# Another order for the first 24 steps of a fused clustered-attention and expert kernel

## The chip, the cores and the metric

The kernel runs on one core of a Trainium2 chip. The metric is the device time of one execution, in microseconds (us). Five queues of instructions run side by side, each strictly in order: TensorE (PE in the profile, its weight loads PEld), VectorE (DVE), ScalarE (ACT), GpSimd (POOL) and SyncE (SP, which here only issues transfers). SPq and ACTq in a row stand for a transfer being issued by that engine's queue.

## The reference, cut to what matters

```python
q_assign = argmax(q_n . c_n)   # 16 clusters a head; k_assign likewise
mask = q_assign[:, :, :, None] == k_assign[:, :, None, :]
scores = where(mask, q k^T / sqrt(D), -1e9)
attn = softmax(scores) @ v                 # 4 batches, 8 heads, 768 tokens, D = 64
x = attn as 3072 rows of 512
out = top-2-of-8 gated experts(x, w1, w2)  # 512 -> 1024 -> 512, relu
```

q, k and the centroids are normalised for the assignment alone.

## The kernel before, in words

Attention is done for 16 pairs of heads, in 192 score steps: pair p, head s of the pair, block kc of 128 keys is step 12p + 6s + kc. A step's `scores` makes two tiles of 128 keys x 384 queries on TensorE (operands A and B, one after the other into the same tile) and has ScalarE take the exponential of each; `split_p` has GpSimd make the second half of the result; `values` multiplies with v four to nine steps later. The score tiles, and those of most helpers, are the six buffers `ring` of PSUM; the seventh writer waits for the reader of the first.

Ahead of its first score a pair needs a preparation, called *pair work* here:

- `scales`: two sums of squares of q and k (ScalarE), a floor, a spread over partitions (TensorE) and a last part of five VectorE instructions that gives the powers of two to scale by. The list holds them in this order.
- `a_turn` and `a_halves` (together `a_split`), four times: three transposes on TensorE, then a high half (ScalarE) and a low half (VectorE) of the turned q or k, into the tile `hl`. That tile has one buffer for pairs 0, 2, 3 and on; pair 1 alone uses another one.
- `b_place`: ten transfers that copy parts of hl into the operands A[p % 3] and Bt[p % 3].
- `a_sims`: 36 short matmuls of the halves with the centroids `wh`, into the tile `aux`; five VectorE instructions on it (`max1`, `ge`, `ky`, `max2`, `eq`) that end in a one-hot; `a_mask`, which turns that on TensorE and writes `mk` from ScalarE; and `b_mask`, four transfers of mk into rows of A, two on SP's queue and two on ScalarE's. 
- `b_max`, for each of twelve row blocks: two matmuls and two VectorE reductions of 128 x 384 that give minus the largest masked score; `b_neg`, three short VectorE instructions, which use columns of `aux` too; and `b_negT`, a transpose, a ScalarE copy and a transfer into Bt. Pair 0 does b_neg and b_negT for each of its heads, the other pairs once for both.

The pair's scores need A with its mask and Bt with its maxima. `load_qk` loads q and k of four heads (two pairs) at a time; `load_v`, `v_sizes`, `v_scale` and `v_split` do the like for v.

The order of all of this is written by hand. `at(step, f)` files f under a third of a step, rounded to the nearest; within one third the order is that in which the calls were filed. A loop then goes through the steps from the first negative one on and issues, in each: what was filed for the first third, the step's `scores`, a `split_p`, the second third, `values`, and the last third. This order is the order on every queue. The times come from the table `AT`, by pair: `first` for pair 0 and offsets (`sec`, `thr`, `place1`, `scales1`, `bmax1`) for pairs 1 and 2. Before, the preparation of pairs 0 and 1 and most of that of pair 2 stands ahead of step 0: pair 2's squares at step -14, its a_split from -5.2 to -3, its b_place at -1.2, pair 1's mask at -12.1 and three row blocks of b_max of pair 0's second head ahead of step 0 or in its first third.

After attention the experts run (lines 949 to 1288), TensorE's matmuls L1230 and L1270 above all.

Of the kernel before, what the change touches and what calls it, by code (L numbers as in the profile page):

```python
# [9 lines left out]
F32 = mybir.dt.float32  # L10
# [4 lines left out]
AF = mybir.ActivationFunctionType  # L15
OP = mybir.AluOpType
# [9 lines left out]

AT = dict(
    ahead=6,
    first={'scales': [-6.667] * 5, 'place': -2.333, 'sims': [-3.333, -2.667], 'max1': -2.333, 'ge': -2.333, 'max2': -2.333, 'eq': -1.333, 'mask': -1.0, 'bmask': -1.0, 'ky': -2.333, 'split': [-5.333, -5.0, -5.333, -4.0], 'bmax': [3.667, 22.667], 'bstep': [1.0, 0.667], 'neg': [9.0, 26.667], 'negT': [9.333, 27.333]},
    L=4, qk=-20.667, v=-8.667,  # L30
    vscale=-0.667, vsplit=10.667, vstep=1.0, split=[-4.667, -3.667, -4.0, -3.333], place=-0.667,
    sims=[2.0, 2.667], scales=[-14.333, -13.333, -13.0, -10.0, -8.667], scales1=2.0, max1=3.333, ge=3.667, max2=4.333, eq=4.667, mask=6.333, bmask=6.333,
    bmax=9.333, neg=20.333, negT=22.0, zero=31.0, zstep=12.0, zlist=21.0, v1=4.0, store=2.667, turn=6.667, glog=12.0,
    xh=1.333, xh0=4.0, pause=4.0, list=[34.0, 34.0, 19.0], lstep=[2.0, 2.0, 1.1667], bstep=1.0,
    gate=[13.667, 13.667, 6.333], am=5.333, amstep=0.333, xs=6.0, ky=4.0, cut=[13, 20], gplace=[30.0, 30.0, 14.333],
    vd=[1, 1, 2, 3, 4, 5], sec=-6.0, qf=[0, -4.0], place1=4.333,
    fv=[{'v': -5.0, 'vscale': 13.0, 'am': 24.333, 'amstep': 0.333, 'vsplit': 25.333, 'vstep': 2.0},
        {'v': 9.0, 'vscale': 11.667, 'am': 13.333, 'amstep': 0.333, 'xs': 14.0, 'vsplit': 15.0, 'vstep': 1.0}],
    wmax=42, thr=0.333, bmax1=14.667, bstep1=0.5)


def rap(tensor, offset, dims):
# [3 lines left out]
class Kernel:  # L46
# [171 lines left out]
    def centroids(self):  # L218
        nc, D, C = self.nc, self.D, self.C
        self.early = self.wk.tile([128, 2, 384], F32, name="pe", bufs=6).rearrange("p a n -> p (a n)")  # L220
        o = 128 + 4 * C
        c1 = self.early[:, o:o + D]
        c2 = self.c2 = self.early[:, o + D:o + 3 * D].rearrange("p (a d) -> p a d", d=D)
        nc.sync.dma_start(c1, self.cent.rearrange("h c d -> (h c) d"))
        self.constants()
        n = self.early[:, o + 3 * D:o + 3 * D + 3]
        nc.vector.tensor_mul(c2[:, 0, :], c1, c1)
        nc.vector.reduce_sum(n[:, 0:1], c2[:, 0, :], axis=X)
        self.rnorm(n[:, 0:1], n[:, 1:3])
        nc.vector.tensor_scalar(c2, c1[:, None, :].to_broadcast([128, 2, D]), n[:, 0:1], None, op0=OP.mult)  # L230

    def c_turn(self):
        nc, H, C = self.nc, self.H, self.C
        HC = H * C
        p = self.ps()
        nc.tensor.transpose(p[:, :128], self.c2.rearrange("p a d -> p (a d)"), self.ident)
        for a in range(2):
            r = slice(64 * a, 64 * a + 64)
            src = p[r, :HC].rearrange("p (h c) -> p h c", c=C)
            hi, lo = (self.wh[r, :, i, C * a:C * a + C] for i in range(2))  # L240
            nc.scalar.activation(hi, src, AF.Copy, scale=64.0)
            nc.vector.scalar_tensor_tensor(lo, src, 64.0, hi, op0=OP.mult, op1=OP.subtract)
        self.early = self.c2 = None

    def attention(self, ctx):
        nc, tc = self.nc, self.tc
        B, H, S, D, NJ = self.B, self.H, self.S, self.D, self.NJ
# [9 lines left out]
        NP = B * H // 2  # L257
# [8 lines left out]
        def at(step, f, *a):  # L266
            sched.setdefault(divmod(round(3 * step), 3), []).append((f, a))
# [6 lines left out]
        T = AT  # L274
        for p in range(NP):
            b, hp = divmod(p, H // 2)
            w = 12 * (p - 2)
            if hp == 0:
                for g in range(2):
                    at(w + T["qk"] + 24 * g + (0 if b else T["qf"][g]), self.load_qk, b, g)  # L280
                    v = w + 24 * g
# [4 lines left out]
                    if g:  # L286
                        fs = self.x_scale(b)
                        chain(v + V["xs"] - (4 if b else 0), 1.0 if b else 0.333, fs[:-1])
                        at(v + V["xs"] + (2.667 if b else 3.333), fs[-1])
                    for h in range(0, 4, 2):  # L290
                        at(v + V["vsplit"] + V["vstep"] * (h + 0.667), self.v_split, b, g, h)
            P = T["first"] if p == 0 else T
            w += (0, T["sec"], T["thr"])[p] if p < 3 else 0
            if p == 0:
                for i in range(4):
                    at(w - 7.0, self.a_turn, p, i // 2, i % 2)
            if p < 2 or p % 2 == 0:
                fs = self.scales(p, 2 if p < 2 else 4)
                for x, f in zip(P["scales"], fs):
                    at(w + x + (T["scales1"] if p == 1 else 0), f)  # L300
            for i in range(4):
                at(w + P["split"][i], self.a_halves if p == 0 else self.a_split, p, i // 2, i % 2)
            if p == 0:
                at(w + P["sims"][0], self.c_turn)
            at(w + P["place"] + (T["place1"] if p == 1 else 0), self.b_place, p)
            for s in range(2):
                at(w + P["sims"][s], self.a_sims, p, s)
            for k, f in (("max1", self.a_max1), ("ge", self.a_ge), ("ky", self.a_ky), ("max2", self.a_max2),
                         ("eq", self.a_eq), ("mask", self.a_mask), ("bmask", self.b_mask)):
                at(w + P[k], f, p)  # L310
            if p == 0:
                for s in range(2):
                    for j in range(NJ):
                        at(w + P["bmax"][s] + P["bstep"][s] * j, self.b_max, p, s, j)
                    at(w + P["neg"][s], self.b_neg, p, s, 1)
                    at(w + P["negT"][s], self.b_negT, p, s, 1)
            else:
                w = 12 * (p - 2)
                bm, bs = (T["bmax1"], T["bstep1"]) if p == 1 else (T["bmax"], T["bstep"])
                for s in range(2):  # L320
                    for j in range(NJ):
                        at(w + bm + bs * (6 * s + j), self.b_max, p, s, j)
                at(w + T["neg"], self.b_neg, p, 0, 2)
                at(w + T["negT"] + (T["thr"] if p == NP - 1 else 0), self.b_negT, p, 0, 2)
            w = 12 * (p - 2)
            z = w + 36 + L
            if p + 1 < NP:
                at(z + T["xh"] + (T["xh0"] if p == 0 else 0), self.x_halves, p)
                at(z + T["store"] + (T["xh0"] if p == 0 else 0), self.store_x, p)
                turn, glog = (T["store"], 6.333) if p == NP - H // 2 - 1 else (T["turn"], T["glog"]) if p < NP - 2 else (5.0, 8.0)  # L330
# [3 lines left out]
            if hp == H // 2 - 1:  # L334
                if b + 1 == B:
                    continue
                fs = self.g_gate(b)
                chain(z + T["gate"][b], 0.333, fs[:8])
                for i, f in enumerate(fs[8:self.GP]):
                    x = T["gate"][b] + 2.667 + (0.333 if b < 2 else 0.1667) * i  # L340
# [3 lines left out]
                    at(z + T["list"][b] + T["lstep"][b] * j, self.g_list, b, j)  # L344
        at(17.667, self.x_early)
        at(T["zlist"], self.zero_list)
        at(-13, self.exp_table)
        at(10.667, self.load_gate)
        chain(13.667, 0.667, self.gate_halves())
        for i in range(self.N // 256):  # L350
# [18 lines left out]
            at(z - 7 + i, self.turn_x, 0, i)  # L369
        at(z - 8, self.open_x)  # L370
        for i in range(2):
            nc.gpsimd.memset(self.oh[i], 0.0)
        nc.gpsimd.memset(self.nm, 0.0)
        self.fixed_init(0)
        at(-14.4, self.fixed_init, 1)
        at(-8.4, self.fixed_init, 2)
        self.at = at
        for t in range(min(sched)[0], z + L + 2):
            u = t - L
# [8 lines left out]
            if 0 <= u < z:  # L388
                p, s, kc = u // 12, (u % 12) // 6, u % 6
# [5 lines left out]

    def fixed_init(self, i):
        nc = self.nc
        nc.gpsimd.memset(self.A[i][64:96], 0.0)
        nc.gpsimd.memset(self.Bt[i][96:128], 0.0)
        nc.gpsimd.memset(self.Bt[i][96:98, 0], 1.0)  # L400
        nc.gpsimd.memset(self.Bt[i][96:97, 0], MASK)

# [181 lines left out]
    def b_place(self, p):  # L584
        hl, A, Bt = self.st[p]["hl"], self.A[p % 3], self.Bt[p % 3]
        for a in range(2):
            r = 64 * a
            cs = slice(384 * a, 384 * a + 384)

            self.dma(A[0:64, :, :, cs], hl[r:r + 64, 1:3])  # L590
            self.dma(A[96:128, 0, :, cs], hl[r:r + 32, 3])
            self.dma(A[96:128, 1, :, cs], hl[r:r + 32, 2])
            self.dma(Bt[0:64, :, :, cs], hl[r:r + 64, 0:2])
            self.dma(Bt[64:96, :, :, cs], hl[r + 32:r + 64, 2:4])

# [735 lines left out]
```

## Time and profile before

| | |
|---|---|
| Median of three runs | 1013.66 us (1013.41 to 1014.27) |
| The profiled execution's own time, and its span | 1013.59 us, 1011.8 us |
| Mean granted TensorE clock | 0.976 of full speed |
| Busy share of the span | PE 92%, DVE 65%, ACT 47%, POOL 56% |
| First exponential of step 0, step 24 | 44.79 us, 100.18 us |

Times in rows count from the first instruction. A row of a timeline has start, duration (from the first to the end of the last of the merged instructions), engine, line, operation, tiles written and read, count, and in brackets how long the engine had idled and what ended that. The names are the program's tiles: `mm` is b_max's, `mk` the mask, `nt` the maxima, `pe` the exponentials, `pl` split_p's, `junk` the squares, `A<-hl` a transfer of b_place.

### The profile page before, as it was taken

What the parts mean: (1) busy time and instruction counts of PE and PEld (TensorE: products, weight loads), DVE (VectorE), ACT (ScalarE), POOL (GpSimd) and SP (SyncE); (2) the same over time, 40 slices, a digit from 0 to 9 for tenths busy, and PEclk for the clock granted to TensorE, in tenths of its full rate; (3) what the DMA queues carried; (4) which work ended last, traced back from release to release, by engine and by line L of the source; (5) the groups of instructions that cost most, each with busy time, mean ns of one, the idle gap of its engine ahead of it and who ended that gap; (6) DMA issues with size and microseconds to landing.
All of it is one profiled execution on the core that took longest, in us unless ns stands there. A gap on an engine that the chain in (4) does not pass through costs nothing.

```text
span 1011.8 us, 22606 instructions
## 1 busy us (share of the span) xinstructions
PE 928.7 (92%) x8825; PEld 560.4 (55%) x8825; DVE 660.6 (65%) x1485; ACT 473.4 (47%) x896; POOL 565.7 (56%) x608
## 2 busy tenths in 40 slices
PE   4588989898899987889999999999999999999997
PEld 3356666666666664668555445455454454554543
DVE  6688777888678876897556465365564654655631
ACT  4578788888787865674032224123131241231310
POOL 9268797979997899853456125242261252422312
PEclk7699999999999998999999999999999999999999
DMA  6543767666667444668377645655665356555201
GB/s 178 125 118 89 194 156 185 183 165 145 179 153 189 119 95 98 204 152 176 109 150 242 137 142 167 140 174 149 173 193 140 126 165 152 172 151 155 73 24 46
DMA packets 181905, 148.84 MB, mean 147 GB/s; under 512 B 93543, under 2 KB 159079, under 8 KB 181794
## 3 DMA queue, kind: packets, MB, share of 16 engines
q1 hardware_dynamic: 167990, 110.73, 43.8%
q0 software_dynamic: 13296, 36.38, 11.7%
q8 instruction: 70, 1.15, 0.5%
q10 hardware_dynamic: 508, 0.25, 0.1%
q14 instruction: 41, 0.34, 0.1%
HBM read 81.80 MB, written 26.12 MB: 107 GB/s over the span
## 4 chain that ended last, share of the span: by engine, by line
PE 57%; POOL 10%; DVE 9%; issue 9%; ACT 6%; DMA 4%; SPq 0%; ACTq 0%; POOLq 0%; DVEq 0%
PE ring L1230 21%; PE ring L1270 20%; POOL pl L653 6%; PE ring L641 5%; ACT pe L642 3%; DVE mm L613 3%; PE ring L611 2%; POOL tbl L899 2%; DMA B<-nt 2%; PE av L670 1%; PE av L676 1%; PE av L672 1%; POOL out L1283 1%; PE ring L1260 1%; DVE pl L653 1%
## 5 line engine op out<-in xcount | busy, mean ns | idle before, releaser
L653 POOL TENSOR_TENSOR pl<-pe 128x768 f16<-128x768 f32 x171 | 247.9, 1468 | 47.4 <-ACT pe L642 41.9
L1230 PE MATMUL ring<-xT,w1t 128*128 128x404 f16 (+2 forms) x1632 | 267.1, 324 | 0.0
L1270 PE MATMUL ring<-w2t,hT 128*128 128x512 f16 x1152 | 250.8, 379 | 0.5 <-DVE w2t L1166 0.5
L642 ACT ACTIVATE pe<-ring,sc 128x384 f32<-128x384 f32 x384 | 200.0, 577 | 69.1 <-PE ring L641 62.0
L613 DVE TENSOR_REDUCE mm<-ring 128x1 f32<-128x384 f32 x384 | 192.1, 549 | 44.6 <-PE ring L611 44.0
L1283 POOL DMA_INDIRECT out<-yo,idx x52 | 58.7, 1129 | 285.4 <-DVE yo L1279 209.3
L1230 PEld LDWEIGHTS <-w1t 128*128 128x128 f16 x1632 | 157.4, 97 | 106.4 <-issue 2.5
L1270 PEld LDWEIGHTS <-hT 128*128 128x128 f16 x1152 | 112.4, 98 | 135.0 <-issue 1.2
L1239 ACT ACTIVATE hT<-ring 128x404 f16<-128x404 f32 (+2 forms) x136 | 57.6, 469 | 202.1 <-PE ring L1230 201.9
L641 PE MATMUL ring<-B 128*128 128x384 f16 x384 | 127.2, 332 | 3.6 <-DMA B<-nt 3.6
L641 PE MATMUL ring<-A 128*128 128x384 f16 x384 | 126.8, 330 | 3.6 <-ACT pe L642 2.1
L611 PE MATMUL ring<-A 128*128 128x384 f16 x384 | 105.2, 334 | 16.5 <-ACT pe L642 8.0
L1240 DVE SCALAR_TENSOR_TENSOR hT<-ring,hT 128x404 f16<-128x404 f32 (+2 forms) x136 | 66.7, 529 | 73.5 <-ACT hT L1239 73.5
L1279 DVE SCALAR_TENSOR_TENSOR yo<-ring,lsw,xt 128x512 f32<-128x512 f32 (+1 forms) x49 | 36.7, 748 | 110.2 <-PE ring L1270 104.3
L670 PE MATMUL av<-vv,pe 128*128 128x65 f16 x1152 | 96.9, 194 | 7.5 <-DVE xt L685 7.4
L672 PE MATMUL av<-vv,pe 128*128 128x64 f16 x1152 | 96.9, 193 | 0.0
L670 PEld LDWEIGHTS <-pe 128*128 128x128 bf16 x1152 | 83.7, 98 | 22.9 <-issue 9.3
L1165 ACT ACTIVATE w1t<-stg,ws 128x1024 f16<-128x1024 f32 x32 | 34.5, 1139 | 121.2 <-DVE ws L170 121.2
L672 PEld LDWEIGHTS <-pe 128*128 128x128 bf16 x1152 | 78.4, 99 | 11.3 <-issue 4.7
L676 PE MATMUL av<-vv,pl 128*128 128x65 f16 x1152 | 66.8, 194 | 5.6 <-POOL pl L653 4.2
L1210 POOL DMA_INDIRECT xh<-xs,idx x52 | 56.4, 1085 | 16.5 <-issue 15.0
L1154 DVE TENSOR_REDUCE wm<-stg 128x1 f32<-128x1024 f32 x56 | 65.5, 1208 | 0.0
(227 smaller groups left out, 1171.0 us busy)
## 6 DMA issues: line engine op xcount, KB each, us to landing
stg<-in_moe_w SPq DMA_DIRECT2D x64, 512.0 KB
vt<-in_v SPq DMA_DIRECT2D x8, 768.0 KB
out<-zt SPq DMA_DIRECT2D x12, 512.0 KB
A<-hl SPq DMA_DIRECT2D x30, 192.0 KB
B<-hl SPq DMA_DIRECT2D x30, 192.0 KB
xs<-xh SPq DMA_DIRECT2D x15, 384.0 KB
qk<-in_q SPq DMA_DIRECT2D x7, 768.0 KB
qk<-in_k SPq DMA_DIRECT2D x7, 768.0 KB
```

The costliest lines, as they stand in the source:

```text
L611: nc.tensor.matmul(t, A[:, 0, s, j * 128:j * 128 + 128], A[:, 1, s, n * 384:n * 384 + 384], start=True, stop=True)
L613: nc.vector.tensor_reduce(st["mm"][:, c, n:n + 1], t, axis=X, op=OP.max, negate=True)
L641: nc.tensor.matmul(t, M[:, 1 - qi, s, ks], M[:, qi, s, ns], start=not qi, stop=bool(qi))
L642: nc.scalar.activation(pe[:, n], t, AF.Exp, bias=math.log(64.0), scale=st["sc"][:, 4:5])
L653: (nc.vector if last else nc.gpsimd).tensor_tensor(lo, pe, hi, op=OP.subtract)
L670: nc.tensor.matmul(av[:, j, :], ph[:, js], vv[:, hh, kj, 64:129], start=(kc == 0 and j == 0), stop=False, skip_group_check=True)
L672: nc.tensor.matmul(av[:, j, :64], ph[:, js], vv[:, hh, kj, 0:64], start=False, stop=False, skip_group_check=True)
L676: nc.tensor.matmul(av[:, j, :], pl[:, js], vv[:, hh, kj, 64:129], start=False, stop=(kc == NJ - 1), skip_group_check=True)
L1230: nc.tensor.matmul(p, self.w1t[:, wi, c, f * 128:f * 128 + 128], self.xT[:, c, xi, n0:n1], start=(i == 0), stop=(i == 3 * ND - 1))
L1240: nc.vector.scalar_tensor_tensor(h1, x, 0.0, h0, op0=OP.max, op1=OP.subtract)
L1270: nc.tensor.matmul(p, self.hT[:, hi, f, t * 128:t * 128 + 128], self.w2t[:, wi, f], start=(i == 0), stop=(i == 3 * NF - 1))
L1283: i = nc.gpsimd.indirect_dma_start(out=self.out, out_offset=bass.IndirectOffsetOnAxis(ap=en[:r], axis=0), in_=yo[:r], in_offset=None, boun ...
```

## The change

Three things change.

1. The times of pairs 0, 1 and 2 come from a new list `early`, one table a pair, in place of `first` and the offsets. Ahead of step 0 stay: pair 0's preparation with b_max, b_neg and b_negT of its first head, and pair 1's up to `eq`. Behind it go: b_max, b_neg, b_negT of pair 0's second head (steps 0.3 to 4.3), pair 1's mask (1.3) and b_max (4.3 to 9.8), and all pair work of pair 2: squares at 0.7 and 1.7, a_split from 4.3 to 5.3, b_place at 5.7, a_sims at 6.7, its mask at 11 and b_max from 13.7 to 21. a_split of pair 3 stays at 7.3 to 8.7. load_qk of the second pair of pairs moves, by `qf`, to just before pair 0's mask, v_sizes is the last thing ahead of step 0, and c_turn is cut in two, with its transposes ahead of the spread of pair 0 and its halves (`c_halves`) ahead of a_halves.
2. The scaled copies of the centroids are two ScalarE instructions in place of one of VectorE; memsets of zero in `oh`, A and Bt are written as half as many 4-byte elements.
3. For pair 0, three of b_place's ten transfers are issued from ScalarE's queue.

```diff
     ahead=6,
-    first={'scales': [-6.667] * 5, 'place': -2.333, 'sims': [-3.333, -2.667], 'max1': -2.333, 'ge': -2.333, 'max2': -2.333, 'eq': -1.333, 'mask': -1.0, 'bmask': -1.0, 'ky': -2.333, 'split': [-5.333, -5.0, -5.333, -4.0], 'bmax': [3.667, 22.667], 'bstep': [1.0, 0.667], 'neg': [9.0, 26.667], 'negT': [9.333, 27.333]},
+    early=[
+        dict(turn=-20.0, cturn=-19.667, scales=[-20.0, -20.0, -19.333, -19.333, -19.0], chalves=-18.667,
+             split=[-18.333] * 4, place=-18.0, sims=[-17.667] * 2, max1=-17.333, ge=-17.333, ky=-17.333, max2=-17.333,
+             eq=-17.333, mask=-15.667, bmask=-15.667, bmax=[-14.333, 0.333], bstep=[0.0, 0.667], neg=[-14.0, 4.0],
+             negT=[-13.667, 4.333]),
+        dict(scales=[-17.0, -17.0, -16.667, -16.333, -15.333], split=[-15.0] * 4, place=-14.667, sims=[-14.0] * 2,
+             max1=-13.0, ge=-13.0, ky=-13.0, max2=-13.0, eq=-13.0, mask=1.333, bmask=1.333, bmax=4.333, bstep=0.5,
+             neg=10.0, negT=10.333),
+        dict(scales=[0.667, 1.667, 2.0, 3.667, 4.0], split=[4.333, 4.667, 5.0, 5.333], place=5.667, sims=[6.667, 7.0],
+             max1=8.0, ge=8.333, ky=8.667, max2=9.0, eq=9.333, mask=11.0, bmask=11.0, bmax=13.667, bstep=0.667,
+             neg=21.333, negT=22.333)],
...
-    vd=[1, 1, 2, 3, 4, 5], sec=-6.0, qf=[0, -4.0], place1=4.333,
-    fv=[{'v': -5.0, 'vscale': 13.0, 'am': 24.333, 'amstep': 0.333, 'vsplit': 25.333, 'vstep': 2.0},
+    vd=[1, 1, 2, 3, 4, 5], qf=[0, 5.167],
+    fv=[{'v': -5.0, 'vscale': 11.667, 'am': 24.333, 'amstep': 0.333, 'vsplit': 25.333, 'vstep': 2.0},
...
-        nc.vector.tensor_scalar(c2, c1[:, None, :].to_broadcast([128, 2, D]), n[:, 0:1], None, op0=OP.mult)
+        for a in range(2):
+            nc.scalar.activation(c2[:, a], c1, AF.Copy, scale=n[:, 0:1])
 
     def c_turn(self):
+        self.ct = self.ps()
+        self.nc.tensor.transpose(self.ct[:, :128], self.c2.rearrange("p a d -> p (a d)"), self.ident)
+
+    def c_halves(self):
...
         for a in range(2):
             r = slice(64 * a, 64 * a + 64)
-            src = p[r, :HC].rearrange("p (h c) -> p h c", c=C)
+            src = self.ct[r, :H * C].rearrange("p (h c) -> p h c", c=C)
...
-            P = T["first"] if p == 0 else T
-            w += (0, T["sec"], T["thr"])[p] if p < 3 else 0
+            P = T["early"][p] if p < 3 else T
+            w = 0 if p < 3 else w
...
-        at(-13, self.exp_table)
+        at(-16, self.exp_table)
...
-            nc.gpsimd.memset(self.oh[i], 0.0)
+            nc.gpsimd.memset(self.oh[i].bitcast(F32), 0.0)
...
-        at(-14.4, self.fixed_init, 1)
-        at(-8.4, self.fixed_init, 2)
+        at(-18.333, self.fixed_init, 1)
+        at(-12, self.fixed_init, 2)
...
-        nc.gpsimd.memset(self.A[i][64:96], 0.0)
-        nc.gpsimd.memset(self.Bt[i][96:128], 0.0)
+        nc.gpsimd.memset(self.A[i][64:96].bitcast(F32), 0.0)
+        nc.gpsimd.memset(self.Bt[i][96:128].bitcast(F32), 0.0)
...
-            self.dma(A[0:64, :, :, cs], hl[r:r + 64, 1:3])
-            self.dma(A[96:128, 0, :, cs], hl[r:r + 32, 3])
-            self.dma(A[96:128, 1, :, cs], hl[r:r + 32, 2])
+            queue = self.nc.scalar if a and p == 0 else None
+            self.dma(A[0:64, :, :, cs], hl[r:r + 64, 1:3], queue)
+            self.dma(A[96:128, 0, :, cs], hl[r:r + 32, 3], queue)
+            self.dma(A[96:128, 1, :, cs], hl[r:r + 32, 2], queue)
```

The rest of the diff has the loop take b_max, b_neg and b_negT of pairs 1 and 2 from the same tables.

## Rows read from the trace of the kernel before

**Rows 1.** Chain of waits, whole run: start, duration, what held the chain.

```profile
460.63 7.87 PE ring L1230 x72
```

**Rows 2.** Timeline of ScalarE: the first exponentials.

```profile
44.79 1.22 ACT L642 ACTIVATE pe<-ring,sc 128x384 f32<-128x384 f32 x2 [2.16 <-PE ring L641]
```

**Rows 3.** Windows; busy us (count) of PE, PEld, DVE, ACT, POOL; PEclk; DMA.

```profile
0.00:44.79 44.79, 20.51 (x149) 13.76 (x150) 28.02 (x75) 19.77 (x37) 27.64 (x29) 0.66 0.55 150
44.79:75.16 30.37, 26.12 (x312) 16.63 (x311) 26.27 (x63) 23.21 (x43) 20.33 (x14) 0.99 0.48 127
75.16:100.18 25.02, 21.33 (x327) 15.46 (x327) 20.67 (x62) 20.52 (x40) 21.63 (x20) 1.00 0.35 88
...
75.16:95.10 19.94, 16.34 (x253) 12.00 (x253) 15.95 (x52) 15.44 (x31) 16.55 (x15) 1.00 0.39 96
...
46.60:68.10 21.50, 18.15 (x218) 11.81 (x217) 18.79 (x45) 15.02 (x28) 15.66 (x11) 1.00 0.54 153
```

**Rows 4.** Timeline of VectorE.

```profile
4.42 2.38 DVE L230 TENSOR_SCALAR pe<-pe 128x128 f32<-128x128 f32 x1
7.38 0.43 DVE L495 TENSOR_REDUCE ring<-ring 128x2 f32<-128x256 f32 x1 [0.59 <-PE ring L489]
...
8.33 0.20 DVE L499 TENSOR_SCALAR sc<-ring,sc 128x1 f32<-128x1 f32 x1
...
14.38 0.56 DVE L549 TENSOR_REDUCE mx<-aux 128x24 f32<-128x384 f32 x1 [1.18 <-PE aux L545]
...
23.71 5.66 DVE L613 TENSOR_REDUCE mm<-ring 128x1 f32<-128x384 f32 x12
...
68.02 1.14 DVE L525 SCALAR_TENSOR_TENSOR hl<-ring,sc,hl 128x384 f16<-128x384 f32 x2
```

**Rows 5.** Timeline of GpSimd.

```profile
4.06 2.65 POOL L398 MEMSET A<- 32x3072 f16 x1
...
46.10 1.47 POOL L653 TENSOR_TENSOR pl<-pe 128x768 f16<-128x768 f32 x1 [17.08 <-ACT pe L642]
```

**Rows 6.** Timeline of ScalarE ahead of step 0.

```profile
18.39 0.90 ACT L577 ACTIVATE mk<-ring,ms 128x768 f16<-128x768 bf16 x1 [5.51 <-PE ring L575]
...
30.83 1.20 ACTq L582 DMA_DIRECT2D B<-nt  x1
...
35.28 1.28 ACT L139 ACT_TABLE_LOAD   x1
```

**Rows 7.** Timelines of SP and TensorE around load_qk, and SP's waits there.

```profile
21.26 0.51 SPq L411 DMA_DIRECT2D qk<-in_k  x1
...
22.05 1.07 PE L611 MATMUL ring<-A 128*128 128x384 f16 x4 [1.13 <-DMA A<-mk]
...
28.76 0.60 SPq L582 DMA_DIRECT2D A<-xt  x1
...
SPq L582 <- DMA qk<-in_k: 1.4, 1, 1.4
SPq L582 <- DMA A<-xt: 0.4, 1, 0.4
```

**Rows 8.** Timeline of ScalarE in steps 6 to 12.

```profile
60.34 0.90 ACT L577 ACTIVATE mk<-ring,ms 128x768 f16<-128x768 bf16 x1
61.27 1.53 ACTq L582 DMA_DIRECT2D A<-mk  x2
...
72.76 1.03 ACT L642 ACTIVATE pe<-ring,sc 128x384 f32<-128x384 f32 x2
73.69 1.48 ACT L178 ACTIVATE junk<-vt 128x1536 bf16<-128x1536 f32 x1
```

**Rows 9.** b_place of pair 2 on SP, and a like landing in the chain.

```profile
42.65 1.97 SPq L582 DMA_DIRECT2D A<-hl  x3
...
48.05 1.29 SPq L582 DMA_DIRECT2D B<-hl  x2
...
109.03 2.67 DMA B<-hl
```

## What I expected, before the change was run

> **What bounds the kernel now.** I read the chain of waits first [rows 1]: from 460 us on it is TensorE in the expert layers, back to back, and the change touches nothing there. What the first 24 steps gain or lose therefore reaches the end almost undiminished. Next the first exponential of step 0, which begins at 44.79 us [rows 2], and windows cut there and at the first ones of steps 12 and 24 [rows 3]: 44.79 us of preparation, 30.37 us for steps 0 to 11, 25.02 us for steps 12 to 23. In the preparation no engine is busy for more than 28.02 us: it is a chain of dependent work. In steps 0 to 11 VectorE is busy for 26.27 of 30.37 us. ScalarE has 23.21, and 2.7 more in which it issues two mask transfers (1.53 [rows 8]) and one of the maxima (1.20 in a like place [rows 6]). In steps 12 to 23 four engines lie between 20.5 and 21.6 of 25.02.
>
> **The change up to the first score.** Four edits there are worth little.
> - Centroids scaled by ScalarE: a VectorE instruction of 2.38 us goes, but VectorE's next one starts at 7.38 and waits for TensorE [rows 4]. The two ScalarE instructions cost between 0.2 and 0.4 us each and are mostly hidden by the wait for k. With c_turn now ahead of the spread I take +0.3 us. The 2.38 us end with a GpSimd memset [rows 5]; the Trainium skill (SBUF — State Buffer, Who interferes with whom) says VectorE in a two-port mode is blocked for a GpSimd instruction's whole length. By that rule some 2 us of waiting go, and were VectorE the path here the sum would be 2 lower. By the rows they lie beside TensorE's work and bring nothing.
> - Memsets with half the elements: GpSimd's first score work starts at 46.10 after 17 idle us [rows 5]. Between nothing and half of 2.65 us each, all covered: 0.
> - Three transfers on ScalarE's queue: SP is 1.95 us sooner with its part, ScalarE pays some 0.75 each (1.53 for two [rows 8]). The mask lands later than these operands, so 0 as long as ScalarE is back for the mask; it is, below.
> - Squares of pair 1 behind pair 0's halves: two times some 0.9 us (half of the 1.48 that twice the columns take [rows 8], and the read-out) leave the path, and c_halves (four short instructions, about 0.6) enters it.
>
> Together the halves end near 12.2 us and the cluster products near 12.8, against 14.35 before the first VectorE maximum at 14.38 [rows 4]. The mask activation then started 4.0 us later, at 18.39 [rows 6]. Now ScalarE issues three transfers, does two squares and a table load of 1.28 us and is free at about 17.2; the mask is done at 18.1 (19.29 before).
>
> Then a queue takes it back. load_qk(0,1), issued behind the mask's transfers before, is now ahead of them on SP (its third-step rounds to the same one, and it is entered first). In the trace the k half, issued at 21.26, landed only when the waiting SP transfer could go at 28.76: 7.5 us. A small operand transfer issued at 23.01 behind it held SP up again until about 29.8 [rows 7]. With SP's part of b_place gone by 16.2 (seven issues of some 0.65 each, as in [rows 9], from 11.6 on), k is issued at 16.9 and lands at 24.4, and SP's half of the mask at 24.8 (22.05 before [rows 7]). The Trainium skill (DMA: Bandwidth & Descriptors, Queues, rings and completion order) has each engine take one queue's descriptors in ring order, SP and ScalarE each with rings of their own: by it ScalarE's half overtakes the load and SP's doesn't, as the held operand row shows.
>
> From there: twelve reductions of 5.66 us in all [rows 4] end at 30.9 (the first 0.45 after the landing). b_neg, negT and its copy took 1.46 from the last reduction to the issue at 30.83 [rows 4, 6]. Pair 1's cluster products now stand between b_neg and negT on TensorE and write the tile that b_neg reads: 1.2 us, as VectorE's wait for the like products shows (1.18 [rows 4]). The issue takes 1.0 (1.20 before), v_sizes 1.5 [rows 8], and it ends when the maxima have landed. The first exponential comes at 36.1: **-8.7 us**. Bounds: if the mask isn't held, halves of pair 1 set the start and it is 33.4 (-11.4); if the load lands 1.4 us later, 37.5 (-7.3).
>
> **Steps 0 to 11.** What moved behind the first score is real work: on ScalarE two squares of 1536 columns (1.5 each), a mask with two DMA issues (2.5, from 60.34 to 62.80), four halves (about 0.5 each, as VectorE's), a floor (0.1): 7.6 us in all [rows 4, 8]. And it comes in lumps on queues that run in order.
> - Head: three pairs of exponentials (0.93 each, from 72.76 to 73.69 [rows 8]), two squares, mask and issues stand in line on ScalarE: 8.4 us. The scores of step 3 need the buffers of step 2, and b_max(0,1,5) stands behind them on TensorE, so VectorE gets it at 9.4.
> - Middle: from there to b_neg(1) VectorE has 26 reductions at 0.47 (12.3), eight halves at 0.53 (1.14 for two, with their overlap: 4.3), five cluster operations at 0.55 (2.7), and twelve short instructions at 0.2 with one each of 0.43 and 0.56 (the last of pair 2, two b_neg, one output scaling: 3.4): 22.7 [rows 4]. Before, the like stretch from 46.60 to 68.10 held 18.79 of work in 21.50 [rows 3], 2.7 idle, a good part of it the mask and its issues, which now lie outside; I take 1.5.
> - A new wait: hl is one buffer for pairs 2 and 3. b_place(2) now ends in step 5, and pair 3's first half, in step 7, rewrites hl. The ten transfers took from 42.65 to 49.34 to issue and the last some 2.5 more to land (2.67 in a like place) [rows 9]: 9.2 us. Between the two lie two steps, 5.1 us at 2.53 a step. ScalarE waits 4.1, with the exponentials of step 8 queued behind it, and VectorE with it. Before, eight steps lay between, and it cost nothing.
> - Tail: after b_neg(1), negT and its copy (0.6), ScalarE still owes a square, mask and issues, floor, one exponential and v_sizes: 6.7.
>
> Sum 9.4 + 22.7 + 1.5 + 4.1 + 0.6 + 6.7 = 45.0, against 30.37: **+14.6 us**. Without the hl wait +10.5, without it and other idle time +9.0; with 1.5 us more idle and 1.4 from TensorE's lower clock (1.2 GHz; the granted mean was 0.66 in the preparation [rows 3]) in the first steps, +17.5.
>
> **Steps 12 to 23.** Four row blocks of b_max(2), done ahead of step 12 before, now come behind it: 3.8 us on VectorE, and two halves (1.1) move ahead of b_neg(2), which step 24 needs. Before, VectorE was busy 15.95 of 19.94 us up to b_neg(2) [rows 3]; of these 4.0 idle some are filled. Between +0.9 and +4.9, I take **+3.0** (the blocks are now as dense as in the middle above). What follows b_neg(2), from 95.10 to step 24 at 100.18, stays.
>
> Sum: -8.7 + 14.6 + 3.0 = +8.9 us on the profiled execution's 1013.59; the median of the runs, 1013.66, is the same within 0.1. **1022.5 us**, with a range of its own of 1013 to 1028 (all lower bounds at once would give 1012, all upper ones 1029).
>
> **Rivals.**
> - The work fills gaps (faster). If ScalarE never idles, steps 0 to 11 take 23.21 + 2.7 + 7.6 = 33.5 us instead of 45.0, and steps 12 to 23 +0.9: -8.7 + 3.1 + 0.9 = -4.7, 1008.9 us. For it: VectorE's total hardly grows (-2.8 for fewer reductions, +3.2 for halves and last), and the preparation had idle time everywhere. Against it: the lumps above, with six score buffers between the engines. It decides once steps 0 to 11 stay under 38.2 us.
> - No hl wait: the transfers land sooner, or step 7 comes late anyway: 4.1 less, 1018.4. The code's one buffer speaks against it.
> - The mask isn't held behind load_qk: 2.7 less, 1019.8. The 7.5 us of [rows 7] speak against it. So does the ring order that the Trainium skill states on the page named above.
> - Gain and loss cancel: hl wait and mask hold both absent, and steps 12 to 23 at +0.9: -11.4 + 10.5 + 0.9 = 0, 1013.6 us.
> - More of it: the lower clock in steps 0 to 5, TensorE being starved in the head, or a later nt in step 6 as well: 1027.
>
> **How the numbers follow.** My sum 0.40, no hl wait 0.12, mask not held 0.10, more 0.07: slower 0.69. Cancelling 0.09. Filled gaps 0.22. What can be told from no change here is about 0.2%, 2 us. The range 1008 to 1027 takes in the faster rival's centre and leaves its lower half and the upper tail out, under 2 in 10; both signs hold chance, so the sum's own range is given above.
>
> **What would show it.** Right: first exponential between 35 and 38 us; b_max(0,0) starting only when SP's mask lands behind k; ScalarE near 9 us for the first three steps; a wait of pair 3's first half or its VectorE partner for b_place(2)'s transfers of 3 to 5 us; step 12 later than 77 and step 24 later than 103. Wrong: step 12 before 73 us would make the order of lumps harmless and the sum's middle terms too large; a first exponential under 34 would drop the queue term; no wait ahead of pair 3's first half would drop 4.1.

## The result, and the profile after

Beside four runs of the kernel before, with a median of 1013.96 us (1013.41 to 1014.61), four runs of the changed kernel had a median of 1025.08 us (1024.03 to 1025.95). The ratio is 1.0109, with a 95% interval of 1.0091 to 1.0126: the change costs 11 us. The profiled execution took 1025.16 us, with a span of 1023.4.

The windows of the changed kernel, cut as in [rows 3] at the first exponential of step 0, of step 12 and of step 24; the three below them cut steps 0 to 11 and 12 to 23 further (same columns):

```profile
0.00:37.11 37.11, 14.68 (x124) 10.77 (x125) 21.10 (x61) 14.58 (x29) 19.31 (x29) 0.94 0.62 174
37.11:81.88 44.77, 31.89 (x329) 20.93 (x328) 27.28 (x66) 29.27 (x54) 20.33 (x14) 0.82 0.35 91
81.88:111.53 29.65, 24.95 (x335) 16.94 (x335) 25.36 (x70) 21.21 (x40) 23.30 (x21) 0.94 0.32 83
...
37.11:46.53 9.42, 7.39 (x40) 3.42 (x38) 7.75 (x23) 7.78 (x15) 2.93 (x2) 0.86 0.31 89
46.53:74.69 28.16, 20.17 (x216) 14.29 (x216) 19.10 (x41) 16.48 (x30) 16.15 (x11) 0.77 0.36 101
...
81.88:107.65 25.77, 21.22 (x284) 14.47 (x283) 21.69 (x62) 17.82 (x34) 19.41 (x19) 0.93 0.34 87
```

The preparation is 7.68 us shorter than in [rows 3], steps 0 to 11 are 14.40 longer, steps 12 to 23 4.63 longer: together +11.35 at step 24. The chain of waits shows that nearly all of it reaches the expert layers. The row that answers to [rows 1]:

```profile
471.59 7.86 PE ring L1240 x72
```

It starts 10.96 us later than its counterpart. All lines of the changed file lie nine or ten further down (exponential L642 is now L652, halves L524 and L525 are L533 and L534, row maxima L613 are L623).

The timeline of ScalarE in the changed kernel holds the three places that the prediction spoke of: the head (37.11 to 45.59), the wait for hl (63.84), the tail (75.51 to 81.88).

```profile
37.11 1.03 ACT L652 ACTIVATE pe<-ring,sc 128x384 f32<-128x384 f32 x2
38.04 1.48 ACT L188 ACTIVATE junk<-qk 128x1536 bf16<-128x1536 f32 x1
...
39.50 1.05 ACT L652 ACTIVATE pe<-ring,sc 128x384 f32<-128x384 f32 x2
40.43 0.91 ACT L586 ACTIVATE mk<-ring,ms 128x768 f16<-128x768 bf16 x1
41.42 1.48 ACTq L591 DMA_DIRECT2D A<-mk  x2
42.95 1.48 ACT L188 ACTIVATE junk<-qk 128x1536 bf16<-128x1536 f32 x1 [1.60 <-POOL pl L663]
...
44.66 1.04 ACT L652 ACTIVATE pe<-ring,sc 128x384 f32<-128x384 f32 x2
45.59 0.93 ACT L476 ACTIVATE vt<-vt,am 128x768 f32<-128x768 f32 x1
...
57.89 1.05 ACT L652 ACTIVATE pe<-ring,sc 128x384 f32<-128x384 f32 x2
63.84 1.05 ACT L533 ACTIVATE hl<-ring,sc 128x384 f16<-128x384 f32 x2 [4.90 <-DMA B<-hl]
64.79 1.05 ACT L652 ACTIVATE pe<-ring,sc 128x384 f32<-128x384 f32 x2
...
75.51 0.27 ACT L639 ACTIVATE nt<-ring 24x128 f16<-24x128 f16 x1 [2.41 <-PE ring L637]
75.69 1.47 ACT L188 ACTIVATE junk<-qk 128x1536 bf16<-128x1536 f32 x1
...
77.15 0.88 ACT L586 ACTIVATE mk<-ring,ms 128x768 f16<-128x768 bf16 x1
78.06 1.27 ACTq L591 DMA_DIRECT2D A<-mk  x2
...
79.49 1.03 ACT L652 ACTIVATE pe<-ring,sc 128x384 f32<-128x384 f32 x2
80.42 1.48 ACT L188 ACTIVATE junk<-vt 128x1536 bf16<-128x1536 f32 x1
...
81.88 1.99 ACT L652 ACTIVATE pe<-ring,sc 128x384 f32<-128x384 f32 x4
```

Between the exponential at 57.89 and the halves at 63.84 ScalarE does nothing; the releaser is the transfer that still reads hl. The exponential of step 8 at 64.79 stood behind the halves in ScalarE's own queue. The same waits seen from VectorE:

```profile
26.40 5.67 DVE L623 TENSOR_REDUCE mm<-ring 128x1 f32<-128x384 f32 x12 [3.48 <-PE ring L621]
...
33.94 0.56 DVE L558 TENSOR_REDUCE mx<-aux 128x24 f32<-128x384 f32 x1 [1.21 <-PE aux L554]
...
37.83 1.02 DVE L623 TENSOR_REDUCE mm<-ring 128x1 f32<-128x384 f32 x2 [0.95 <-PE ring L621]
...
39.23 4.88 DVE L623 TENSOR_REDUCE mm<-ring 128x1 f32<-128x384 f32 x10
...
47.12 0.56 DVE L623 TENSOR_REDUCE mm<-ring 128x1 f32<-128x384 f32 x1 [0.77 <-PE ring L621]
48.25 0.56 DVE L623 TENSOR_REDUCE mm<-ring 128x1 f32<-128x384 f32 x1 [0.57 <-PE ring L621]
50.86 0.62 DVE L534 SCALAR_TENSOR_TENSOR hl<-ring,sc,hl 128x384 f16<-128x384 f32 x1 [2.05 <-ACT hl L533]
...
58.32 1.02 DVE L623 TENSOR_REDUCE mm<-ring 128x1 f32<-128x384 f32 x2 [0.63 <-PE ring L621]
64.46 0.62 DVE L534 SCALAR_TENSOR_TENSOR hl<-ring,sc,hl 128x384 f16<-128x384 f32 x1 [5.11 <-ACT hl L533]
```

### The profile page after: what moved, and what is told of

The parts are those of the page before. It is cut to its first block, busy times and chain, and to the rows that moved or that the text cites. A ratio compares the mean times of both kernels' runs of the same rounds, so it can differ in the third digit from the quotient of the medians.

```text
span 1023.4 us, 22600 instructions
## 1 busy us (share of the span) xinstructions
PE 931.0 (91%) x8825; PEld 563.0 (55%) x8825; DVE 659.0 (64%) x1484; ACT 474.8 (46%) x898; POOL 554.6 (54%) x608
## 4 chain that ended last, share of the span: by engine, by line
PE 57%; DVE 10%; POOL 9%; issue 9%; ACT 6%; DMA 4%; SPq 1%; ACTq 0%; POOLq 0%; DVEq 0%
PE ring L1240 21%; PE ring L1280 20%; POOL pl L663 5%; PE ring L651 4%; ACT pe L652 3%; DVE mm L623 3%; DMA B<-nt 2%; PE ring L621 2%; PE av L680 2%; PE av L686 2%; PE av L682 1%; POOL tbl L909 1%; POOL out L1293 1%; PE ring L1270 1%; DVE pl L663 1%
## 5 line engine op out<-in xcount | busy, mean ns | idle before, releaser
L652 ACT ACTIVATE pe<-ring,sc 128x384 f32<-128x384 f32 x384 | 200.2, 578 | 63.8 <-PE ring L651 57.8
L623 DVE TENSOR_REDUCE mm<-ring 128x1 f32<-128x384 f32 x384 | 192.5, 548 | 47.8 <-PE ring L621 46.1
```

What stands on the lines that cost most here:

```text
L623: nc.vector.tensor_reduce(st["mm"][:, c, n:n + 1], t, axis=X, op=OP.max, negate=True)
L652: nc.scalar.activation(pe[:, n], t, AF.Exp, bias=math.log(64.0), scale=st["sc"][:, 4:5])
```

## The experiments

Twelve runs followed, the changed kernel once more and eleven variants, each beside the kernel before on the same chip. The chips were not that of the first result: the kernel before had medians of 1065.9 us beside the first four, 1065.4 beside the next four, 1049.7 beside the three after (the same chip as for the four, later) and 1014.7 beside the last. The difference arises late: in the first experiment TensorE's granted clock was 0.96 from 460 to 935 us, where the first chip had 1.00. So I compare ratios, and above all the times of the first exponentials, which lie ahead of it. They are from each run's timeline of ScalarE (us). The kernel before has a profile on the first chip alone, so a difference from its times holds the difference between chips too.

| kernel | step 0 | steps 0 to 11 | steps 12 to 23 | step 24 at | ratio to before, 95% interval |
|---|---|---|---|---|---|
| before | 44.79 | 30.37 | 25.02 | 100.18 | |
| changed | 37.11 | 44.77 | 29.65 | 111.53 | 1.0109, 1.0091 to 1.0126 |
| changed, again (c0) | 37.59 | 44.44 | 28.60 | 110.63 | 1.0092, 1.0070 to 1.0114 |
| own buffer (e1) | 38.16 | 40.12 | 28.59 | 106.87 | 1.0052, 1.0034 to 1.0071 |
| mask first (e2) | 33.76 | 45.26 | 29.63 | 108.65 | 1.0060, 1.0038 to 1.0081 |
| early squares (e3) | 38.72 | 43.01 | 28.58 | 110.31 | 1.0082, 1.0055 to 1.0109 |
| local edits alone (e4) | 44.74 | 31.51 | 25.01 | 101.26 | 0.9998, 0.9982 to 1.0014 |
| e1, e2 and e3 (e5) | 33.98 | 38.50 | 31.41 | 103.89 | 1.0011, 0.9995 to 1.0028 |
| third pair back (e6) | 42.03 | 37.27 | 25.65 | 104.95 | 1.0031, 1.0012 to 1.0050 |
| e6 and e2 (e7) | 37.88 | 36.18 | 25.75 | 99.81 | 0.9998, 0.9977 to 1.0019 |
| e7, packed (e8) | 33.68 | 37.50 | 25.76 | 96.94 | 0.9943, 0.9900 to 0.9986 |
| e8, masks on SP (e9) | 33.62 | 35.67 | 24.95 | 94.24 | 0.9925, 0.9888 to 0.9961 |
| changed, masks on SP (e10) | 37.35 | 41.00 | 27.22 | 105.57 | 0.9996, 0.9956 to 1.0037 |
| before, masks on SP (e11) | 43.87 | 29.84 | 24.77 | 98.48 | 0.9972, 0.9962 to 0.9981 |

The changed kernel ran twice. The two differ by 0.5 us at step 0, 0.3 in steps 0 to 11 and 1.1 in steps 12 to 23. e1 and e10, in which nothing ahead of step 0 differs from it, have step 0 at 38.16 and 37.35: a single profile tells step 0 to about 1 us.

> The changed kernel once more, beside the three others. Every account: ratio to the kernel before 1.009 to 1.0125, first exponential 37 to 38.7 us, steps 0 to 11 44 to 45.5, steps 12 to 23 28.5 to 29.7.

All four numbers came within these ranges. The windows of the repeat, cut at the same three places (same columns as above):

```profile
0.00:37.59 37.59, 14.86 (x124) 10.70 (x125) 21.10 (x61) 14.57 (x29) 19.31 (x29) 0.65 0.61 172
37.59:82.03 44.44, 33.29 (x329) 22.00 (x328) 27.28 (x66) 29.27 (x54) 20.32 (x14) 0.83 0.34 92
82.03:110.63 28.60, 23.86 (x335) 16.01 (x335) 25.07 (x70) 21.25 (x40) 23.32 (x21) 1.00 0.34 86
```

**The wait for hl (e1).** Pair 2's halves go into the tile that pair 1 used.

```diff
-            st["hl"] = (self.gp.tile([128, 4, 2, 384], F16, name="xt", bufs=1) if p == 1 else
+            st["hl"] = (self.gp.tile([128, 4, 2, 384], F16, name="xt", bufs=1) if p in (1, 2) else
```

> The changed kernel with the third pair's halves in the second pair's buffer (free by then), so that the fourth pair's halves no longer rewrite a buffer that is being copied out. My account: the 4.9 us wait ahead of the fourth pair's first half goes, steps 0 to 11 take 40 to 41 us in place of 44.8, and the end comes 3.5 to 5 us sooner, about 1020.5. Rival: the wait only stood in for another one (TensorE's clock, a full ring of score buffers, VectorE's backlog), the work between is what counts, and less than 1.5 us come back.

ScalarE's timeline there, at the halves that waited 4.90 us:

```profile
59.06 1.05 ACT L652 ACTIVATE pe<-ring,sc 128x384 f32<-128x384 f32 x2
60.01 0.58 ACT L533 ACTIVATE hl<-ring,sc 128x384 f16<-128x384 f32 x1
```

The wait is gone, and steps 0 to 11 are 4.3 to 4.7 us shorter than in the two changed runs. The rival, that another wait stood behind it, falls.

**The mask behind the load (e2).** The second operand load is issued behind the mask on SP, and nothing else in any queue's order differs.

```diff
-    vd=[1, 1, 2, 3, 4, 5], qf=[0, 5.167],
+    vd=[1, 1, 2, 3, 4, 5], qf=[0, 5.334],
```

> The changed kernel with the second operand load issued on SP's queue right behind the first pair's mask instead of right ahead of it. My account: the mask lands near 22 us as before, the first row maximum is held by the second pair's halves alone, the first exponential comes 2 to 2.7 us sooner (34.4 to 35.1 in place of 37.1), and the end follows, 1022.5. Rival one: since ScalarE's half of the mask landed as late as SP's, the late landing is not the queue's order, and nothing moves. Rival two: the first exponential comes sooner, but the load lands 1 to 2 us later, the third pair's squares wait for it, and less than 1 us reaches the end.

TensorE's timeline at the first row maximum, in the changed kernel and then in this one:

```profile
25.88 2.40 PE L621 MATMUL ring<-A 128*128 128x384 f16 x7 [6.00 <-DMA A<-mk]
```

```profile
21.42 1.04 PE L621 MATMUL ring<-A 128*128 128x384 f16 x4 [1.61 <-DMA A<-mk]
22.66 3.79 PE L621 MATMUL ring<-A 128*128 128x384 f16 x8 [0.20 <-DVE xt L534]
```

TensorE waits for the mask 4.5 us less long. VectorE then goes from the second pair's halves (L534) to the first reduction without a wait, so these halves set the start, as the account had it:

```profile
20.94 2.19 DVE L534 SCALAR_TENSOR_TENSOR xt<-ring,sc,xt 128x384 f16<-128x384 f32 x4 [2.85 <-ACT xt L533]
23.05 5.66 DVE L623 TENSOR_REDUCE mm<-ring 128x1 f32<-128x384 f32 x12
```

The first exponential comes 3.3 to 3.8 us sooner, more than the 2.7 expected, and 2.0 to 2.9 of it are still there at step 24. Both rivals fall.

**The squares (e3).** Pair 2's two squares run in ScalarE's wait of 11.9 us ahead of step 0.

```diff
-        dict(scales=[0.667, 1.667, 2.0, 3.667, 4.0], split=[4.333, ...
+        dict(scales=[-14.0, -14.0, 2.0, 3.667, 4.0], split=[4.333, ...
```

> The changed kernel with the third pair's two squares back ahead of the first score, in ScalarE's wait of 11.9 us. My account: the first exponential stays at 37.1, the line of ScalarE's work in the first three steps is 3 us shorter (5.5 in place of 8.5), steps 0 to 11 are 2.5 to 3 us shorter, and the end comes at about 1022.3. Rival: VectorE's work, or the lower clock of TensorE, sets the start of the stretch behind the head, and less than 1 us comes back.

Steps 0 to 11 shrink by 1.4 to 1.8 us, not by 3. Where a square had stood, ScalarE now waits for the score:

```profile
38.72 1.03 ACT L652 ACTIVATE pe<-ring,sc 128x384 f32<-128x384 f32 x2
41.04 1.22 ACT L652 ACTIVATE pe<-ring,sc 128x384 f32<-128x384 f32 x2 [1.29 <-PE ring L651]
```

Half of my account stands: the head is bound by ScalarE and TensorE in turn, not by ScalarE alone. TensorE's matmuls of 128 x 384 took 0.53 us there up to 43.0, 0.33 from 43.2 on, so its lower clock, which the rival names, can have a part in that wait; no run shows how much.

At the end next to nothing is shown: the first exponential came at 38.72, not at 37.1, and step 24 is only 0.3 to 1.2 us sooner than in the two changed runs; the interval of the ratio takes in both of theirs. The later start isn't the edit's as far as the rows tell: the mask was issued at 19.09 and waited for to 27.49 (18.51 and 25.88 in the changed kernel), and the moved squares run behind that issue.

**The local edits alone (e4).** The kernel before with only the ScalarE scaling of the centroids, the 32-bit memsets and the three transfers on ScalarE's queue (the diff ahead of the prediction shows them).

> The kernel before with the four edits alone that leave the order of steps as it was: centroids scaled by ScalarE, memsets as 32 bit, three of the first pair's operand transfers on ScalarE's queue. My account: all lie beside other work, 0 with at most 0.5 us either way, 1013.2 to 1014.5. Rival one: the 2.38 us instruction of VectorE was on the path of the preparation, and 1.5 to 2 us go, about 1012. Rival two: ScalarE's three issues, 2.6 us, delay the second pair's squares and everything behind them, 1 to 2 us more.

They are worth nothing that can be measured, as expected. Step 0 stays at 44.74; that steps 0 to 11 are 1.1 us longer in this profile isn't borne out by the ratio.

**The three fixes together (e5).**

> The changed kernel with the third pair's halves in their own buffer, the load behind the mask, and the third pair's squares in ScalarE's early wait, all three. My account: the three terms lie at different places of the path and add up: first exponential near 34, steps 0 to 11 near 38.5 (44.8 less 4.6 less 1.8), steps 12 to 23 near 28.6, step 24 near 101; with it the loss is all but gone, ratio 1.000 to 1.002. Rival: behind each of them stands the same VectorE work, the three hide one another, and the ratio stays above 1.004.

Step 0 and steps 0 to 11 add up to within 0.3 us: 33.98 against 33.76 in e2, and 38.50 against 38.36 (44.77 less 4.65 in e1 and 1.76 in e3). Steps 12 to 23 are 2.8 longer than in the repeat, so step 24 comes at 103.89 and not near 101:

```profile
72.48:103.89 31.41, 26.92 (x335) 18.09 (x335) 25.82 (x70) 21.60 (x40) 23.39 (x21) 0.89 0.30 79
```

e1, e2 and e3 have the same order in these steps; they took 28.59 and 28.58 us at a granted clock of 1.00 (e1 and e3) and 29.63 at 0.94 (e2). The length goes with the clock there, though no run changed the clock by itself. The ratio lies in the range of my account and away from the rival's.

**The third pair back (e6), and with the mask first (e7).** Pair 2's preparation returns to its old steps; e7 has the edit of e2 too.

```diff
-        dict(scales=[0.667, 1.667, 2.0, 3.667, 4.0], split=[4.333, 4.667, 5.0, 5.333], place=5.667, sims=[6.667, 7.0],
...
+        dict(scales=[-14.0, -13.0, -12.667, -9.667, -8.333], split=[-4.333, -3.333, -3.667, -3.0], place=-0.333,
+             sims=[2.333, 3.0], max1=3.667, ge=4.0, ky=4.333, max2=4.667, eq=5.0, mask=6.667, bmask=6.667, bmax=9.333,
+             bstep=1.0, neg=20.333, negT=22.0)],
```

> The changed kernel with the third pair's preparation alone put back where it was: squares, halves and copies ahead of the first score, products, mask and maxima at the old steps. The first two pairs keep their new order. My account: the loss is what this pair's work does in the short line behind the first score; the first exponential moves to 41 to 42 us, steps 0 to 11 take 32 to 35, steps 12 to 23 25, step 24 lies at 99 to 102, ratio 0.998 to 1.001. Rival: the second pair's denser maxima and the first pair's second half fill steps 0 to 11 by themselves; they stay over 38 us, steps 12 to 23 near 27, ratio 1.005 or more.

> The last one with the second operand load also behind the first pair's mask on SP's queue. My account: the first exponential comes 2.5 to 3 us sooner than there (38.5 to 39.5), the rest is the same, ratio 0.995 to 0.998, faster than both kernels. Rival: the third pair's squares need this load ahead of the first exponential now, so what the mask gains the load loses; the first exponential stays within 1 us of 41 to 42, ratio 0.998 to 1.001.

In e6, step 0 and steps 12 to 23 came near what was expected, steps 0 to 11 did not: 37.27 lies between the two accounts, step 24 at 104.95 is 3 us later than mine, and the ratio of 1.0031 is just above mine. The third pair is thus worth 5.7 of the 10.45 us that the repeat lies behind the kernel before at step 24. The other 4.8 are still there with that pair put back. In e7 the mask order gives 4.15 us at step 0, and 5.14 at step 24, which comes at 99.81 (100.18 before): with the load behind the mask, the new order of the first two pairs costs nothing at step 24. Its ratio says the same and is my rival's rather than mine: no difference from before. The rival's reason fails all the same, since step 0 did come sooner.

**Packing the preparation (e8).** From e7: v's sizes, pair 2's squares and scale into ScalarE's and VectorE's waits ahead of the first maxima, and pair 1's products behind the maxima's transpose.

```diff
-        dict(scales=[-17.0, ... place=-14.667, sims=[-14.0] * 2,
+        dict(scales=[-17.0, ... place=-14.667, sims=[-13.667] * 2,
-        dict(scales=[-14.0, -13.0, -12.667, -9.667, -8.333], split=[-4.333, ...
+        dict(scales=[-14.333, -14.333, -14.333, -14.0, -14.0], split=[-4.333, ...
-    fv=[{'v': -5.0, 'vscale': 11.667,
+    fv=[{'v': -5.0, 'vscale': 9.333,
```

> The third pair back and the load behind the mask, as in the run before last; now also v's sizes, both squares of the third pair and its scale in the waits ahead of the first maxima, and the second pair's products behind the maxima's transpose on TensorE. My account: ScalarE's line between the maxima and the first score loses 3.2 us (a square and v's sizes), the maxima are sent 1 us sooner; first exponential 34.4 to 35.5, steps 0 to 11 as there (36.2), step 24 at 96 to 97.5, ratio 0.995 to 0.998, faster than both kernels. Rival: the load lands late, the second square holds the maxima's copy on ScalarE, and the first exponential stays above 36.5; ratio 0.998 to 1.001.

Step 0 comes at 33.68, 4.2 us sooner than in e7 and more than expected, with the third pair's preparation ahead of it; the maxima are copied at 29.95 against 30.80. Steps 0 to 11 are 1.3 longer than in e7, where I expected no change, and step 24 lies in the range of my account. The ratio is a little better than my range, and its interval ends below 1: it is faster than both kernels.

**Mask transfers on SP (e9, e10, e11).** Each of the pairs 1 to 3 had half of its mask issued by ScalarE. In e10 and e11 SP issues all of it, in e9 for pairs 2 and 3.

```diff
-                         self.nc.scalar if a and p < 5 else None)
+                         self.nc.scalar if a and p in (0, 4) else None)
```

> The last one with the mask transfers of the third and fourth pair all on SP's queue, which is empty there. My account: ScalarE loses 1.5 us of issuing in steps 7 to 8, where VectorE idles 2.3 us for the fourth pair's halves, and 1.5 in steps 12 to 23; together 1.5 to 3 us sooner than the last one. Rival: neither stands on the path, under 0.5 us.

> The changed kernel with the mask transfers of the second, third and fourth pair all on SP's queue; ScalarE issues none behind the first score. My account: the line of ScalarE's work in the first three steps is 1.5 us shorter (7.0 in place of 8.5), the tail of steps 0 to 11 1.3 shorter, and the stall in steps 12 to 23 1.3 shorter; step 24 2.5 to 4 us sooner, ratio 1.006 to 1.008. Rival: SP sends its halves of the masks one behind the other, they land 1 us later or more, the row maxima start later by what ScalarE gains, and under 1 us is left.

> The kernel before, its order unchanged, with the mask transfers of the second, third and fourth pair all on SP's queue. My account: ScalarE's issuing was on the path in the old order too: 1.5 us ahead of the first score (43.3 in place of 44.8), 1.5 in steps 6 to 8, under 1 in steps 12 to 23; step 24 at 96.4 to 97.5 in place of 100.2, ratio 0.996 to 0.9975; what the run with the packed preparation has beyond that, some 2 to 3 us, is the new order of the first two pairs. Rival one: all of that run's gain came from the queue, step 24 at 94 to 95, ratio 0.993 to 0.995. Rival two: the old order hides ScalarE's issues, under 0.5 us.

The windows of e10, then of e9:

```profile
37.35:78.35 41.00, 30.74 (x327) 20.20 (x326) 27.15 (x66) 29.06 (x55) 20.34 (x14) 0.88 0.36 94
78.35:105.57 27.22, 24.11 (x339) 16.28 (x338) 24.46 (x70) 21.20 (x40) 23.35 (x21) 1.00 0.39 98
```

```profile
0.00:33.62 33.62, 17.34 (x138) 12.51 (x139) 21.80 (x66) 19.85 (x38) 19.33 (x29) 0.75 0.70 192
33.62:69.29 35.67, 26.10 (x322) 17.24 (x322) 30.42 (x70) 24.12 (x45) 20.26 (x14) 1.00 0.42 111
69.29:94.24 24.95, 21.10 (x327) 15.47 (x326) 20.63 (x62) 20.62 (x40) 21.37 (x20) 1.00 0.38 95
```

In the changed kernel this one line gives 5.1 us at step 24 against the repeat (3.4 in steps 0 to 11, 1.4 behind them), more than I expected: the line of the first three steps takes 6.87 us against 8.75 in the repeat, the tail from the maxima's copy on 4.91 against 6.37, each a little more than the 1.5 and 1.3 us of the issues. The ratio's interval, 0.9956 to 1.0037, lies below my range too; 0.9996 is some 10 us under the repeat's 1.0092, twice what step 24 shows, and no row here tells where the rest comes from. ScalarE's busy time hardly moves (29.06 against 29.27): issuing is not counted as busy, so the rows of the windows hide this cost, and only the ACTq rows of the timeline show it. In e9 the edit gives 2.7 us at step 24, as expected, and VectorE is busy for 30.42 of 35.67 us. VectorE's wait for the fourth pair's halves, in e8 and then in e9:

```profile
57.11 0.62 DVE L534 SCALAR_TENSOR_TENSOR hl<-ring,sc,hl 128x384 f16<-128x384 f32 x1 [2.26 <-ACT hl L533]
```

```profile
55.35 0.62 DVE L534 SCALAR_TENSOR_TENSOR hl<-ring,sc,hl 128x384 f16<-128x384 f32 x1 [0.48 <-ACT hl L533]
```

The intervals of their ratios overlap, so it is the rows that show this gain. In e11 the edit gives 1.7 at step 24 and a ratio of 0.9972: the old order paid for the issues too. The ratio lies in my range and below that of no gain; step 24 gained 1 us less than I expected. But the copy of pair 0's first maxima, ahead of all that the edit moves, already came 1.1 us later there (31.59 against 30.49). From this copy to step 24, e11 is 2.8 us shorter. It lies 4.2 us behind e9 at step 24, some 3 of them not from that late start; so much, then, the packed new order is worth beside the queue. The ratios' intervals, which just don't overlap, come from two chips and say it less surely.

## Why the prediction was right, step by step

The forecast of 1022.5 us lies 2.7 under the profiled 1025.16: 1.0 of it in the first score and 1.6 in steps 12 to 23, while steps 0 to 11 came out within 0.2. The range of 1008 to 1027 held both signs, so it is this sum that the account below goes by.

**The first score** was forecast at 36.1 and came at 37.11 (37.59 in the repeat). The chain was the forecast one, with the maxima's start as the place where it ran late: I had the mask at 24.8, and TensorE waited for it to 25.88. That the load in front of it is the cause is shown by e2; the hold was worth 3.3 to 3.8 us, not 2.7, and the bound without it, 33.4, was good (33.76 in e2). The wait for pair 1's products (1.21 against 1.2), the issue (1.19 against 1.0) and v_sizes (1.48) came as in the sum.

**The head.** ScalarE's line took 8.48 us (37.11 to 45.59) against 8.4. But the conclusion drawn from it failed: VectorE did not wait until 9.4 us for b_max(0,1,5). Its twelve reductions ended at 44.11, 7.0 us after the first exponential, and with the squares gone (e3) ScalarE waited for TensorE instead.

**The middle** was 22.7 of work, 1.5 idle and 4.1 of waiting, 28.3 in all, up to b_neg(1). From 46.53 to that point the windows show 28.16, but 19.10 of work and 9.06 idle: the rows give 0.77, 0.57, 2.05, 0.63 and 5.11. The work was 3.6 too high (two of the reductions and the short instructions of pair 2's scale and of pair 0's second b_neg were already done in the head), and the idle time 3.5 too low. The 2.05 is VectorE standing behind pair 2's own halves, which I had not priced. So this sum is right by two errors that cancel.

**The wait for hl** was 4.90 against 4.1, and e1 shows that nearly all of it lay on the path (4.3 to 4.7).

**The tail**, 0.6 and 6.7, took 7.19 (74.69 to 81.88).

**Steps 12 to 23** took 4.63 us more, near the upper bound of 4.9; I had 3.0. In the repeat it was 3.58. The same program at a granted clock of 1.00 (repeat) and 0.94 (first run) differs by 1.05 us there, so about 1 us is not the order's. The place is the forecast one, the reason for 3.0 is not: b_neg(2) ends 25.77 us after step 12 against 19.94 in [rows 3], with 21.69 of work on VectorE against 15.95. The 4.0 us of idle time, some of which the new work was to fill, are still 4.1 (3.3 in the repeat, which ends b_neg(2) after 24.71 with 21.40 of work). Nor did the stretch behind b_neg(2) stay at 5.08: it took 3.88 (3.89 in the repeat). So here too two misses cancel in part.

**The edits at zero** cost and bring nothing (e4). The Trainium skill's rule of VectorE in a two-port mode blocked for a GpSimd instruction's length (SBUF — State Buffer, Who interferes with whom) would have counted only with VectorE on the path; e4, which removes the 2.38 us instruction and leaves step 0 where it was, agrees with the rows' reading. Of the two queues, what the prediction took from the Trainium skill's ring order (DMA: Bandwidth & Descriptors, Queues, rings and completion order) agrees with e2 as to SP's half. That ScalarE's half overtakes the load is wrong here. It was issued on its own queue from 18.51 to 20.01; the packets of each queue from 18.5 to 23 us in the changed kernel, and then from 23 to 24 (SP's is q1, ScalarE's q10):

```profile
q1 hardware_dynamic: 1005, 1.46, 100.2%
```

```profile
q1 hardware_dynamic: 288, 0.26, 94.5%
q10 hardware_dynamic: 96, 0.05, 17.2%
```

So both halves came behind the load. The sum rests on SP's half alone and isn't touched by this.

**The rivals.** The faster one needed steps 0 to 11 under 38.2 us. They took 44.77, and even with the three fixes 38.50. That there would be no wait for hl, or that the mask wouldn't be held, is ruled out by the rows and by e1 and e2; with both of these undone, and the squares moved (e5), the loss is indeed nearly gone, as the cancelling rival had it. No run has those two alone.

What stays open is TensorE's clock. It was granted 0.82 in steps 0 to 11 (0.83 in the repeat) where the kernel before had 0.99, and 1.00 in e9, where VectorE is busy for 30.42 of 35.67 us. In the middle the first run had 0.77; the repeat had 0.88 in the like stretch and was 0.3 us shorter there (27.83 for 28.16). No run changed the clock by itself, so what part of the idle time it caused isn't known. In the preparation it mattered little: the changed kernel had 0.94 in one run and 0.65 in the other, and step 0 differed by 0.5 us, no more than between runs in general.

## What to carry to other kernels

Work that is moved behind the first score is free only if the queues it joins have room at that very place: count each queue's lump, its transfer issues included, and not the engine's mean. Look for what the moved step now sits next to: here one buffer that two pairs share (4 to 5 us in steps 0 to 11) and one load in front of a small transfer (3 to 4 us at step 0, 2 to 3 at step 24) made more than half of a loss that three small edits undo nearly whole by the ratio (e5). When a preparation is a chain of dependent work, as here, first fill the waits that the engines have in it before moving work out of it: e8, which does that, is the first variant faster than the kernel before.

## What the runs showed of the hardware that was not expected

- Issuing a transfer cost ScalarE at least as much as computing one of the halves (0.58 us): two issues took 1.27 to 1.53 us in the rows. Taking six of them away brought step 24 5.1 us forward in the changed kernel, where each pair of them stood ahead of exponentials in ScalarE's queue.
- Mask transfers of 24 KB each, issued behind a load of 2 x 768 KB, were waited for to 25.88 us, and ahead of it to 21.42. Those on ScalarE's own queue fared no better: none of their packets moved before 23.0 us, when the load on SP's queue was nearly through.
- The granted clock in the preparation was 0.94 in one run and 0.65 in another of the same program, and its length differed by 0.5 us.
